# Turning five of seven FFT blocks by DMA instead of on TensorE, in the backward pass of a two-layer SSM and MLP kernel

## The chip, the cores and the metric

The kernel runs on one core of a Trainium2 chip. The core has a matrix engine (PE, with its weight loads shown as PEld), a vector engine (DVE), a scalar engine (ACT), a general engine (POOL) and a sequencer that only issues transfers (SP). SP, ACT and POOL each issue DMAs to a queue of their own; all queues share 16 DMA engines. The metric is the time of one execution on the device in microseconds (us); lower is better.

## The reference, cut to what matters

The reference is a two-layer network and the gradients of its eight inputs. Each layer is an SSM block (a short shift convolution, a product, a long convolution by FFT, a gate) and a SiLU MLP, both behind a layer norm and a residual. All arrays are bf16, with sequence length S = 2048, width D = 448 and hidden width F = 1792.

```python
def _A_ref(q, k, v, shift_k, ssm_k, ssm_D):
    ...
    kv = k_shift * v
    ...
    y_f = kv_f * kf_f[None, :, :, :]
    y = irfft2(y_f, s=(1, L))[:, 0, :S, :]
    y = y + kv * ssm_D[None, None, :]
    return q * y
...
x = x + _A_ref(_layernorm(x), A_k, A_v, A_shift_k, A_ssm_k, A_ssm_D)
x = x + _B_ref(_layernorm(x), B_w1, B_w2)
x = x + _A_ref(_layernorm(x), A_k, A_v, A_shift_k, A_ssm_k, A_ssm_D)
x = x + _B_ref(_layernorm(x), B_w1, B_w2)
...
_out, _vjp = jax.vjp(_f, A_q, A_k, A_v, A_shift_k, A_ssm_k, A_ssm_D, B_w1, B_w2)
```

The outputs are the forward result and the eight gradients. Both layers share their weights, so the gradient of `y`, the output of the long convolution, is summed over the layers and goes back through the FFT once, at the end.

## The kernel before, in words

The program has three parts. `_ssm_prefix` computes the forward long convolution. `Main.run` goes over four chunks of 512 positions and does the forward and backward of both layers; along the way it stores the operands of the weight gradients, turned, in DRAM (`OP_d`, keys a and g per layer), and the normalised inputs n1 and n3 (`N_d`). `_ssm_suffix` takes the gradient of `y` back through the FFT. The change lies in the suffix.

**Stages of the suffix.** Stage 1 of the FFT (`_fft_stage1`, L214) multiplies the 16 rows of the output gradient (`Ysb`) by a matrix and copies the results into the tile A1 (`A1g`); the last four rows run at L1165. Stage 2 needs each 128x128 block of A1 turned. The loop at L1185 does this for seven groups of sixteen blocks: `_turn64` (L222) issues 32 matmuls with the identity into a PSUM tile of the tag `mm`, and a copy (L1189) brings the result to `Z[g]`, a part of the tile `B1v`. DVE or ACT does the copy, by the balancer `_Bal.pick`, which keeps a running total of costs for each. Then `spectrum(cp)` (L1193) does stage 2 on `Z[cp]` at L236 and copies it back on ACT (L1199), and DVE makes a copy with halves swapped (L276). `inverse(cp, ...)` (L1204) forms products with the stored spectra on DVE (L1212, L1213) and runs the first inverse stage (L265), in two chunks per `cp`. Its results go to `B1k`, which is a view of A1's own memory with another layout, and to `B1v_`, each by a copy on ACT (L116). A chunk of `B1k` is a strided set of elements that runs through all of A1. `spec_load(cp)` (L1174) loads the stored spectra on POOL's queue; two buffers rotate for even `cp`, others serve odd `cp`.

**Jobs.** The weight gradients are computed by `Jobs`, a generator whose steps are four matmuls each (L1046). The suffix puts `jobs.run(n)` between its own stages, to keep PE busy. One job run takes a stationary operand `dstat` (512 KB) and does 16 matmuls, against `go` or `X` (L1046, operands a) or against n3 and n1 (operands g). `load` (L1027) issues the DMA for `dstat` from SP's queue at L1038; four buffers rotate. `load_n3` (L1104) loads n3 (1.8 MB) by SP at L1107; it is placed behind the last `dstat` load that the program has issued by then (`issue_after`). A finished weight block is copied by ACT (L1115) and stored by POOL (L1116).

**Order.** PE's order is the program's order, written by hand (`manual_schedule`). On the other engines and queues a planner sets the order, from its own estimate of when each instruction is ready; on the chip each of them then works strictly in that order. Waits are put in where tiles overlap.

Two other places of the kernel turn by DMA, both on SP's queue: L426 in the prefix (two groups of a like tile, SBUF to SBUF) and L595 in `Main.store`.

Of the kernel before, what the change touches and what calls it, by code (L numbers as in the profile page):

```python
# [11 lines left out]
BF16 = mybir.dt.bfloat16  # L12
# [5 lines left out]
P = 128  # L18
# [73 lines left out]
class _Bal:  # L92

    def __init__(self, nc):
        self.nc = nc
        self.load = {"act": 0.0, "dve": 0.0}
# [17 lines left out]
def _copy(nc, eng, out, in_):  # L114
    if eng is nc.scalar:
        return nc.scalar.copy(out, in_)  # L116
    return eng.tensor_copy(out, in_)  # L117
# [18 lines left out]
def kernel(  # L136
# [63 lines left out]
    with tc.manual_schedule(engines={nc.tensor.engine}):  # L200
        with ExitStack() as es:
            Main(k, es).run(ys)
        _ssm_suffix(k)


def _hd(k, shape, name):
    return k.hd.tile(shape, BF16, name=name, tag="hd", bufs=3)


def _load_minv(k, eng):  # L210
    eng.dma_start(out=k.Minvsb[:].rearrange("p n c k -> p (n c k)"), in_=k.minv_h.ap())
# [10 lines left out]
def _turn64(k, pt, i, src):  # L222
    for r in range(2):
        rs = slice(64 * r, 64 * r + 64)
        k.nc.tensor.transpose(pt[:, r, i, :], src[rs], k.ident[rs, rs])
# [776 lines left out]
class Jobs:  # L1002


    def __init__(self, k, main):
        self.k, self.nc, self.main = k, k.nc, main
        self.hd = False
        self.n_ld = self.n_bank = self.n_st = 0
        self.pend = None

    def gen(self):
# [15 lines left out]
    def load(self, key, ft, hd=False):  # L1027
        k, nc = self.k, self.nc
        i = self.n_ld
        self.n_ld += 1  # L1030
        if hd or (self.hd and i % 5 == 4):
            st = _hd(k, [P, NT, P], "dstat")[:]
        else:
            st = self.stat[:, self.n_st % 4]
            self.n_st += 1
        src = k.OP_d[key]
        if key in k.TURNED:
            self.last_ld = nc.sync.dma_start(out=st, in_=src[:, ft, :, :])  # L1038
        else:
            nc.sync.dma_start_transpose(out=st, in_=src[ft, :, :])  # L1040
        return st
# [104 lines left out]
def _ssm_suffix(k):  # L1146
    nc, tc, bal = k.nc, k.tc, k.bal
    jobs = k.jobs
    k_pm = _pm(k.A_k[0])
    v_pm = _pm(k.A_v[0])  # L1150
    psum = k.psum
    mm = dict(tag="mm", bufs=2)
    k.pt = dict(s1=mm, s2=mm, v=mm)
    A1 = k.A1g
    with ExitStack() as es:
# [12 lines left out]
        Z = [B1v_[:, 16 * g:16 * g + 16, :] for g in range(7)]  # L1168
# [3 lines left out]
        A1f = A1[:].rearrange("p a c n s -> p (a c n s)").rearrange("p (a b) -> p a b", b=P)  # L1172

        def spec_load(cp):  # L1174
            lo, hi = cp * 2048, (cp + 1) * 2048
            if cp % 2:
                kk = [kk1[:, i] for i in range(2)]
            else:
                kk = [sp.tile([P, 2048], BF16, name="kk_d", tag="gK", bufs=2)[:] for i in range(2)]
            nc.gpsimd.dma_start(out=kk[0], in_=k.SPEC_d["K"][:, lo:hi])  # L1180
            k.last_sp = nc.gpsimd.dma_start(out=kk[1], in_=k.SPEC_d["KV"][:, lo:hi])
            return kk

        kks = [spec_load(0)]
        for g in range(7):  # L1185
            pt = psum.tile([P, 2, 16, 64], BF16, name="ps_tr", **mm)
            for i in range(16):
                _turn64(k, pt, i, A1f[:, 16 * g + i, :])
            _copy(nc, bal.pick(2048, dve_ns=0.53), Z[g].rearrange("p i (r x) -> p r i x", r=2), pt[:])  # L1189
            jobs.run(1)  # L1190
        kks.append(spec_load(1))

        def spectrum(cp):  # L1193
            xsw = _hd(k, [P, 2048], "xsw_c")
            kk = kks[cp]
            zs = [Zf[cp][:, u * 1024:(u + 1) * 1024] for u in range(2)]
            jobs.run(2)
            for z, ps in zip(zs, _fft_stage2(k, zs, psum)):
                k.last_x = nc.scalar.copy(z, ps[:])  # L1199
            jobs.run(2)  # L1200
            _swap_halves(k, xsw, Zf[cp])
            return kk[0], kk[1], xsw

        def inverse(cp, t):  # L1204
            for u in range(2):
                ci = 2 * cp + u
                o = slice(u * 1024, (u + 1) * 1024)
                prods = []
                for spec_t in (t[1], t[0]):
                    pa, pb = pab[:, 0, n_p[0] % 3], pab[:, 1, n_p[0] % 3]  # L1210
                    n_p[0] += 1
                    nc.vector.tensor_tensor(out=pa, in0=Zf[cp][:, o], in1=spec_t[:, o], op=ALU.mult)  # L1212
                    nc.vector.tensor_tensor(out=pb, in0=t[2][:, o], in1=spec_t[:, o], op=ALU.mult)  # L1213
                    bal.add("dve", 1.9)
                    prods.append((pa, pb))
                jobs.run(6 - u)
                for (pa, pb), B1, cnd in zip(prods, (B1k, B1v_), (True, False)):
                    _fft_inv_stage2_half(k, pa, pb, B1, ci, psum, cnd)

        prev = spectrum(0)  # L1220
        for cp in range(NCI // 2):
            cur = spectrum(cp + 1) if cp + 1 < NCI // 2 else None
            inverse(cp, prev)
            if cp + 2 < NCI // 2:
                kks.append(spec_load(cp + 2))
            prev = cur
            if cp == 0:
                with tc.issue_after(jobs.last_ld.ins):
                    jobs.load_n3()
            if cp == 1:  # L1230
                with tc.issue_after(k.last_sp.ins):
                    nc.gpsimd.memset(gks[:, 16:19, :], 0.0)
                    _load_minv(k, nc.gpsimd)
            if cp == 4:
                with tc.issue_after(k.last_x.ins):
                    nc.scalar.dma_start(out=gks[:, 0:16, :], in_=v_pm)
            if cp == 5:
                ksf = sp.tile([P, 2, J, D // 2], BF16, name="ksf")
                with tc.issue_after(k.last_x.ins):
                    nc.scalar.dma_start(out=ksf[:], in_=k.KS_d[:].rearrange("h p j d -> p h j d"))  # L1240
                skx = ws[:, 0:8 * D].rearrange("p (a b) -> p a b", a=2)
                nc.scalar.dma_start(out=skx[:, 0, :], in_=k.A_shift_k.rearrange("d j -> (d j)").partition_broadcast(P))
                skb = skx[:, 1, :].rearrange("p (j d) -> p j d", j=4)
                nc.vector.tensor_copy(skb, skx[:, 0, :].rearrange("p (d j) -> p j d", j=4))
# [130 lines left out]
```

## Time and profile before

| what | value |
|---|---|
| median of 3 runs | 702.56 us (701.79 to 702.73) |
| profiled execution | 701.8 us |
| its span, first to last instruction | 700.0 us |
| PE busy | 666.0 us, 95% of the span |
| DVE, ACT, POOL busy | 484.1, 432.9, 101.3 us |
| granted TensorE clock | 0.998 |
| bytes by DMA, mean rate | 161.03 MB, 230 GB/s |
| turns in the suffix, L225 | 224 matmuls, 515.6 to 524.7 us |

The profile is of one execution. Its timelines give the start of an instruction in us from the span's start, its duration, and in brackets how long the engine had been idle and what ended that. A name such as `ps_tr<-ident,A1g` is output tile, then inputs. Matmuls are pipelined, so a line's duration reaches over the start of the next; the distance between starts is the time that a group takes. For a DMA the duration is that of issuing it, and its landing is given beside it.

### The profile page before, as it was taken

To read this page: it belongs to the slowest core of one execution; us is meant where nothing else is said; L and a number is where in the kernel's file an instruction comes from. 1 tells how busy PE (TensorE), PEld (TensorE's weight loads), DVE (VectorE), ACT (ScalarE), POOL (GpSimd) and SP (SyncE) were. 2 spreads that over 40 slices of the span, in tenths; PEclk is the share of its full clock that TensorE was granted. 3 is DMA by queue.
4 is the path that set the end of the run, shared out by engine and by line. 5 is a ranking of instruction groups with operands and counts; after the bars stand their busy time and mean duration, and the time that the engine had idled before them with its cause. 6 is when DMAs were issued, how large, how long until landed. Compare 5 with 4: busy or idle time off the path is not lost.

```text
span 700.0 us, 14553 instructions
## 1 busy us (share of the span) xinstructions
PE 666.0 (95%) x5897; PEld 358.8 (51%) x5933; DVE 484.1 (69%) x1131; ACT 432.9 (62%) x522; POOL 101.3 (14%) x173
## 2 busy tenths in 40 slices
PE   6898789999999999999999999999999999999996
PEld 5876545454444444434444444544554555555664
DVE  6688862676889948899578874853946545538991
ACT  5888766968856857769577585223554553554431
POOL 1057110110011100111000100010111211102311
PEclk9999999999999999999999999999999999999999
DMA  8999938459899976698677799959557888966981
GB/s 321 270 298 306 376 84 210 118 107 243 219 231 249 246 200 166 146 240 221 185 165 194 194 242 329 262 172 229 177 208 280 307 279 307 352 188 215 331 293 42
DMA packets 199798, 161.03 MB, mean 230 GB/s; under 512 B 147698, under 2 KB 180213, under 8 KB 198963
## 3 DMA queue, kind: packets, MB, share of 16 engines
q1 hardware_dynamic: 184550, 111.78, 58.8%
q0 software_dynamic: 10368, 36.29, 15.3%
q10 hardware_dynamic: 4812, 12.04, 5.0%
q8 instruction: 46, 0.75, 0.4%
q14 instruction: 22, 0.17, 0.1%
HBM read 66.05 MB, written 54.60 MB: 172 GB/s over the span
## 4 chain that ended last, share of the span: by engine, by line
PE 57%; DVE 22%; issue 10%; ACT 5%; POOL 3%; DMA 2%; POOLq 0%; DVEq 0%; ACTq 0%
PE ps_d L1046 19%; PE ps_n L836 8%; PE ps_h L638 6%; PE ps_g L638 6%; PE ps_o L798 5%; DVE ln_st L301 2%; DVE lb_v L994 2%; PE ps_v L265 2%; PE ps_cv L449 2%; POOL rstd L306 2%; DVE n L309 1%; DVE lb_v L997 1%; DVE lb_v L998 1%; DVE X L802 1%; PE ps_h L642 1%
## 5 line engine op out<-in xcount | busy, mean ns | idle before, releaser
L1046 PEld LDWEIGHTS <-dstat 128*128 128x128 bf16 x896 | 84.0, 98 | 77.8 <-issue 4.0
L836 PE MATMUL ps_n<-w1T,ghT 128*128 128x448 bf16 x448 | 96.6, 353 | 2.0 <-DVE ghT L821 1.7
L798 PE MATMUL ps_o<-w2sb,aT 128*128 128x448 bf16 x448 | 89.2, 353 | 0.7 <-DVE X L802 0.7
L638 PE MATMUL ps_h<-nT,w1sb 128*128 128x512 bf16 (+1 forms) x410 | 83.5, 336 | 2.2 <-ACT Dall L116 1.0
L116 ACT CAST ghT<-ps_g 128x1024 bf16<-128x1024 f32 (+1 forms) x54 | 48.4, 899 | 58.4 <-PE ps_g L642 47.7
L638 PE MATMUL ps_g<-nT,w2T 128*128 128x512 bf16 x317 | 77.9, 379 | 2.2 <-DVE Dall L117 0.5
L836 PEld LDWEIGHTS <-ghT 128*128 128x128 bf16 x448 | 41.4, 98 | 50.7 <-DVE ghT L821 6.7
L798 PEld LDWEIGHTS <-aT 128*128 128x128 bf16 x448 | 43.2, 98 | 41.1 <-issue 2.8
L638 PEld LDWEIGHTS <-w1sb 128*128 128x128 bf16 x420 | 39.2, 98 | 36.7 <-issue 7.2
L781 ACT ACTIVATE aT<-ps_h 128x1024 bf16<-128x1024 f32 (+1 forms) x48 | 44.2, 921 | 19.4 <-PE ps_h L638 10.5
L116 ACT CAST Dall<-ps_h 128x1024 bf16<-128x1024 f32 (+2 forms) x60 | 54.3, 904 | 0.0
L994 DVE SCALAR_TENSOR_TENSOR lb_v<-lb_u,n 128x448 bf16<-128x448 bf16 x60 | 37.2, 620 | 24.6 <-ACT lb_u L840 24.1
L791 ACT ACTIVATE Dall<-Dall 128x1024 bf16<-128x1024 bf16 (+1 forms) x48 | 53.2, 1186 | 0.1
L638 PEld LDWEIGHTS <-w2T 128*128 128x128 bf16 x336 | 31.3, 98 | 42.1 <-issue 7.2
L306 POOL TENSOR_TENSOR rstd<-ln_ve,mhalf 128x2 f32<-128x2 f32 (+1 forms) x24 | 19.9, 831 | 221.1 <-DVE ln_ve L305 221.1
L1046 PE MATMUL ps_d<-X,dstat 128*128 128x448 bf16 x224 | 47.9, 353 | 0.0
L1046 PE MATMUL ps_d<-go,dstat 128*128 128x448 bf16 x224 | 47.2, 353 | 0.0
L1046 PE MATMUL ps_d<-n3m,dstat 128*128 128x448 bf16 x224 | 46.4, 353 | 0.0
L1046 PE MATMUL ps_d<-n1m,dstat 128*128 128x448 bf16 x224 | 46.3, 353 | 0.0
L840 ACT ACTIVATE lb_u<-ps_n,rstd 128x448 bf16<-128x448 f32 x32 | 20.5, 640 | 28.7 <-PE ps_n L836 24.3
L116 ACT CAST A1g<-ps_v 128x1024 bf16<-128x1024 f32 x14 | 14.9, 1066 | 36.5 <-PE ps_v L265 36.5
L802 DVE TENSOR_TENSOR X<-X,ps_o 128x448 bf16<-128x448 bf16 x32 | 19.5, 610 | 21.3 <-PE ps_o L798 21.1
(206 smaller groups left out, 1111.6 us busy)
## 6 DMA issues: line engine op xcount, KB each, us to landing
dstat<-a_d SPq DMA_DIRECT2D x28, 512.0 KB, 5.0
dstat<-g_d SPq DMA_DIRECT2D x28, 512.0 KB, 5.2
a_d<-turned SPq DMA_DIRECT2D x16, 512.0 KB, 3.0
g_d<-turned SPq DMA_DIRECT2D x16, 512.0 KB, 3.2
a_d<-turned SPq DMA_DIRECT2D x16, 384.0 KB, 2.7
g_d<-turned SPq DMA_DIRECT2D x16, 384.0 KB, 3.0
spec_K<-KAB POOLq DMA_DIRECT2D x7, 512.0 KB, 5.4
KAB<-KAB POOLq DMA_DIRECT2D x28, 128.0 KB, 4.6
```

Source lines behind the costliest of these rows:

```text
L116: return nc.scalar.copy(out, in_)
L265: nc.tensor.matmul(pv[:, r ^ (ci & 1), i, :], lhsT=src[ri, i * P:(i + 1) * P], rhs=k.Gsb[ri, g, ri], start=first, stop=not first)
L306: nc.gpsimd.tensor_tensor(out=r[:, lo:hi], in0=ve[:, lo:hi], in1=k.mhalf[:, lo:hi], op=ALU.pow)
L638: self.nc.tensor.matmul(ps, lhsT=w[:, b, ft * P:(ft + 1) * P], rhs=x[:, b], start=(start and b == 0), stop=(stop and b == bs[2]))
L781: self.last_silu = nc.scalar.activation(aT[hh][:, o:o + hi - lo, :], ps(lo, hi), ACT.Silu)
L791: self.nc.scalar.activation(dT[hh][:, o:o + n, :], dT[hh][:, o:o + n, :], ACT.Derivative_silu)
L798: nc.tensor.matmul(po[:, :D], lhsT=aT[ft // 7][:, ft % 7, tl * P:(tl + 1) * P], rhs=self.w2sb[:, ft, :], start=(ft == 0), stop=(ft == NF - 1))
L802: self.last_o = nc.vector.tensor_tensor(out=X[:, t, :], in0=X[:, t, :], in1=po[:, :D], op=ALU.add)
L836: nc.tensor.matmul(pn[:, :D], lhsT=gh[ft // 7][:, ft % 7, tl * P:(tl + 1) * P], rhs=self.w1T[:, ft, :], start=(ft == 0), stop=(ft == NF - 1))
L840: nc.scalar.activation(u0[:], pn[:, :D], ACT.Identity, scale=k.rstd[2 * L + 1][:, t:t + 1], accum_out=cp[:, tl, 0:1])
L994: nc.vector.scalar_tensor_tensor(out=v[:], in0=u0, scalar=-1.0 / D, in1=n_t, op0=ALU.mult, op1=ALU.mult, accum_out=cp[:, 1:2])
L1046: self.nc.tensor.matmul(ps[:, :D], lhsT=st[:, t, :], rhs=mov[:, t, :], start=(first and t == 0), stop=(last and t == NT - 1))
```

## The change

The groups 2 to 6 of A1 are turned by five DMA transposes on SP's queue, issued ahead of the loop; the matmul turns and their PSUM copies stay for groups 0 and 1. The loop still runs seven job steps. From there until the end of the first pass of the inverse loop, `dstat` loads go to POOL's queue instead of SP's; after that pass they go to SP's again. The load of n3 is issued after the second pass instead of the first.

```diff
@@ class Jobs, __init__
         self.n_ld = self.n_bank = self.n_st = 0
+        self.queue = k.nc.sync
         self.pend = None
@@ Jobs.load
         if key in k.TURNED:
-            self.last_ld = nc.sync.dma_start(out=st, in_=src[:, ft, :, :])
+            self.last_ld = self.queue.dma_start(out=st, in_=src[:, ft, :, :])
@@ _ssm_suffix
         kks = [spec_load(0)]
+        jobs.queue = nc.gpsimd
+        for g in range(2, 7):
+            nc.sync.dma_start_transpose(out=Z[g], in_=A1f[:, 16 * g:16 * g + 16, :].rearrange("p a b -> p (a b)"))
         for g in range(7):
-            pt = psum.tile([P, 2, 16, 64], BF16, name="ps_tr", **mm)
-            for i in range(16):
-                _turn64(k, pt, i, A1f[:, 16 * g + i, :])
-            _copy(nc, bal.pick(2048, dve_ns=0.53), Z[g].rearrange("p i (r x) -> p r i x", r=2), pt[:])
+            if g < 2:
+                pt = psum.tile([P, 2, 16, 64], BF16, name="ps_tr", **mm)
+                for i in range(16):
+                    _turn64(k, pt, i, A1f[:, 16 * g + i, :])
+                _copy(nc, bal.pick(2048, dve_ns=0.53), Z[g].rearrange("p i (r x) -> p r i x", r=2), pt[:])
             jobs.run(1)
...
             if cp == 0:
+                jobs.queue = nc.sync
+            if cp == 1:
                 with tc.issue_after(jobs.last_ld.ins):
                     jobs.load_n3()
-            if cp == 1:
                 with tc.issue_after(k.last_sp.ins):
```

## The prediction

> **What bounds the kernel now.** I read the page's chain of waits first, then the PE timeline around the change, then the queues beside it. The chain:
>
> ```profile
> PE 57%; DVE 22%; issue 10%; ACT 5%; POOL 3%; DMA 2%; POOLq 0%; DVEq 0%; ACTq 0%
> ```
>
> It is an average over stages. What a change at L1185 to L1190 is worth is read in that stage, in PE's timeline (start, duration, what):
>
> ```profile
> 514.04 1.68 PE L1046 MATMUL ps_d<-go,dstat 128*128 128x448 bf16 x8
> 515.65 0.64 PE L225 MATMUL ps_tr<-ident,A1g 64*128 64x64 bf16 x32
> 516.23 0.93 PE L1046 MATMUL ps_d<-go,dstat 128*128 128x448 bf16 x4
> 517.09 0.64 PE L225 MATMUL ps_tr<-ident,A1g 64*128 64x64 bf16 x32
> ...
> 524.27 0.64 PE L225 MATMUL ps_tr<-ident,A1g 64*128 64x64 bf16 x32
> 524.85 2.44 PE L1046 MATMUL ps_d<-go,dstat 128*128 128x448 bf16 x12
> 527.22 0.63 PE L236 MATMUL ps_s<-B1v,Gsb 64*64 64x512 bf16 x8
> ```
>
> No idle time stands behind any line: the seven turns and the job matmuls between them follow one another. The table by stretches says the same of what follows (start:end, length, busy PE, PEld, DVE, ACT, POOL, clock, DMA share, GB/s):
>
> ```profile
> 515.20:523.00 7.80, 7.80 (x195) 4.41 (x195) 3.67 (x3) 2.81 (x3) 0.04 (x1) 1.00 0.61 220
> 523.00:531.00 8.00, 8.00 (x108) 4.00 (x105) 3.27 (x5) 5.27 (x5) 0.55 (x1) 1.00 0.42 116
> 531.00:537.00 6.00, 6.00 (x38) 2.94 (x39) 5.88 (x9) 2.36 (x3) 0.54 (x1) 1.00 0.99 404
> ```
>
> PE is full, at full clock, and stays so until 694.9. Its order is written by hand. So work taken out of PE here brings the end nearer by as much, as long as every operand still comes in time: PE, with nothing spare, is also where each late operand shows.
>
> **What goes.** From one turn to the next is 1.435 us (516.23, 517.66, 519.10 and so on for the job matmuls). Four job matmuls without a turn take 0.757 us (16 in 3.03 us, 532.23 to 535.26). So a turn and its two changes of shape cost 0.68 us, and five cost 3.4 us; by the turn's share of the chain alone (0.575 us) it is 2.9. I take 3.4. Five PSUM copies go as well, three on DVE of 1.22 us and two on ACT of 1.87 us. They end no wait of PE, so they are worth nothing; the balancer's totals stand 0.75 us apart before and 0.66 after, so later copies fall to the same engines.
>
> The second half of the kernel hangs on PE's progress: the DVE stretch from 630.6 to 682 begins at a matmul's result, and its loads and stores at PE and DVE events. All of it moves forward together. The tail from 694.9 is unchanged.
>
> **What comes: five transposes on SP.** Each turns 128x2048. Two lines issue that shape:
>
> ```profile
> L595 SPq DMA_TRANSPOSE turned<-aT x32: 1339/1624/3752, 113.7 to 417.4; - x32
> DMA to landing us min/median/max: 3.2/4.0/9.0
> ...
> L426 SPq DMA_TRANSPOSE KAB<-KAB x2: 3603/4920/6238, 20.2 to 26.5; - x2
> DMA to landing us min/median/max: 5.7/8.0/10.4
> ```
>
> (L595's figures mix in blocks of three quarters of the size.) They can start when the last stage-1 copy ends, at 515.2. From below: of two issued one behind the other (306.89 and 308.58) the second, of three quarters, landed 1.37 us after the first, so 1.83 us for a full one; five land by 515.6 + 3.7 + 4 x 1.83 = 526.7. From above: each waits for the one before, at the shorter of L426's two, 5.66 us: 515.6 + 28.3 = 543.9. (The 10.4 us of its first contains loads already queued on SP, the last landing at 26.56.) The five need some 9.2 us of all the DMA engines. Shares of 0.61 and 0.42 leave 7.7 us free by 531, and n3's load, which filled 531 to 537, is gone from there. Loads that now come 3.4 us earlier take some back. I take 531 to 533.
>
> Who needs them? Z[2] is read by PE at 545.28, now 541.9; Z[3] to Z[6] 14 us apart. Earlier is a need that the diff does not show: the first inverse writes A1, which all five transposes read, through B1k:
>
> ```profile
> 538.32 1.07 ACT L116 CAST A1g<-ps_v 128x1024 bf16<-128x1024 f32 x1 [4.33 <-PE ps_v L265]
> 539.28 1.02 ACT L116 CAST B1v<-ps_v 128x1024 bf16<-128x1024 f32 x1
> ...
> 543.25 1.07 ACT L116 CAST A1g<-ps_v 128x1024 bf16<-128x1024 f32 x1 [2.52 <-PE ps_v L265]
> ```
>
> That ACT copy now wants to start at 534.9 and must wait for all five. Behind it on ACT are the B1v copy, a dout copy and the next pair. PE meets the wait when it wants the two `mm` banks for the second inverse chunk, at 542.6 - 3.4 = 539.2; the two copies take 2.0 us, so a landing by 537.2 costs nothing and each us after it one us. I cost it at zero, hidden by 4 us of margin; without that cover it is up to 543.9 - 537.2 = 6.7 us.
>
> **What moves: six dstat loads to POOL.** By PE's runs of 16 they are those used from 519.10, 524.85, 528.54, 532.23, 535.26 and 539.43. Four buffers rotate, so each may be issued when the run four earlier ends: 505.9, 510.1, 513.9, 518.6 and, with the shift, 521.4 and 525.3. Used 3.4 us earlier (the first 0.7), they have 12.5, 11.3, 11.2, 10.2, 10.5 and 10.7 us. POOL's own loads of that size:
>
> ```profile
> kk_d<-spec_K POOLq DMA_DIRECT2D x4, 512.0 KB, 5.7
> kk_d<-spec_KV POOLq DMA_DIRECT2D x4, 512.0 KB, 6.7
> ```
>
> They cost 0.54 us of issue each, 3.2 us in all on an engine that is idle here, and land with 3 us or more to spare. From the other side: 11.82 us, the slowest of them (issued at 589.08), would make each up to 1.6 us late. I take zero. Queued on POOL beside them are dout stores, which wait for ACT for under a us once their run is done, and the second spectrum's load, which waits until 538.5 for DVE:
>
> ```profile
> 534.28 0.54 POOL L1116 DMA_DIRECT2D out_dram<-dout  x1 [8.53 <-ACT dout L1115]
> 538.77 0.54 POOL L1180 DMA_DIRECT2D kk_d<-spec_K  x1 [3.95 <-DVE pab L1213]
> ```
>
> All six can go out well ahead of that load, if the planner puts them there. The next dstat load, on SP from about 529, queues behind transposes instead of beside n3 and is used at 540.2: 11 us.
>
> **What moves: n3.** It goes to SP after the last load of the next pass, about 539.7 instead of 529.16. It landed in 9.2 us; its first use is 577.58, now 574.2. It cannot be late itself. But 1.8 MB, some 4 us of DMA time, enter a stretch with shares of 0.81 to 1.0 (539 to 561). Loads behind it there had 3 to 4 us of spare (issued 550.57, landed 558.84, used 562.5). It is spread over four loads: zero, at worst some 2 us.
>
> **The sum.** Profiled execution: 701.8 us, of which 700.0 is its span. 701.8 - 3.4 = 698.4. The median of three, 702.56, lies 0.76 above it, so 702.56 - 3.4 = **699.2 us** for the median.
>
> **Rivals.**
>
> *A. The overwrite of A1 waits* (slower). If the transposes land one after another, at 543.9, PE stands 6.7 us at the second inverse chunk: 699.2 + 6.7 = 705.9. It turns the gain into a loss from a landing at 540.6 on, that is at over 5.0 us per transpose. For it: L426's issues took 3.6 and 6.2 us, and dstat loads share the DMA engines. Against it: the pairs of L595 overlap. Chance 0.12.
>
> Here a rule of the Trainium skill speaks against the change: the page "VectorE: DVE Perf Modes", section "The three transpose paths", gives a DMA transpose of 128x128 bf16 1309 ns and TensorE 390 ns. As an estimate from that page, a block of sixteen would take 20.9 us and five would land at 620, some 83 us too late. The trace does not agree: sixteen in one DMA land in about 4 us. So that form of A gets 0.01 of its 0.12.
>
> *B. POOL's order* (slower). If the planner puts the last job load behind the second spectrum's, it is issued at 535.9 at the earliest and lands 5.7 us later, at 541.6; PE wants it at 536.0. That is 5.6 us: 704.8. Nothing in the profile shows the new order; for it only that POOL works strictly in order, against it that the load is free ten us earlier. Chance 0.07.
>
> *C. Crowded DMA* (gain partly lost). POOL loads at 11.8 us, transposes landing at 538 to 540, or n3 among the loads around 550 take 1 to 3 us: 700.2 to 702.2. Chance 0.14.
>
> That the change does nothing can be left out: the diff takes matmul turns and copies out under one condition.
>
> **How the numbers follow.** Forecast 0.67 (698.4 to 700.0), C 0.14, A 0.12, B 0.07. Forecast and C hold 0.81, so the range is 698.4 to 702.2; A and B lie beyond it. About 0.2%, 1.4 us, is what a measurement of this kernel can tell from no change. Faster than 701.15: the forecast and nearly half of C, 0.73. Within: the rest of C, 0.08. Slower than 703.97: 0.19.
>
> **What would show it.** Right: two turns at L225 instead of seven, `spectrum`'s first L236 at about 523.8, no idle PE time up to 560, the first A1g copy after it on ACT still released by PE, last transpose landed by 537. Wrong: that copy released by a DMA of B1v and PE idle before the second L265 (A); PE idle at L1046 with POOL waiting at L1180 (B); PE idle at L1046 with dstat landings over 9 us (C).

## The result, and the profile after

The changed kernel takes 709.5 us (median of 6 runs, 705.9 to 717.7); the kernel before took 702.7 us (701.8 to 703.2) in the same rounds. The ratio is 1.0081, 95% interval [1.0056, 1.0106]: slower, where 699.2 us had been forecast. Ratios leave out executions more than 1.5% above the fastest of the same kernel (here one of six, at 717.7 us); medians and ranges take in all. The profiled execution of the changed kernel took 709.26 us, 707.3 of it the span. Its lines lie one or two below those of before: L1047 for the job matmuls, L1188 for the transposes, L1039 for `dstat` loads.

The chain of waits has a new member, SP's queue at 3%, and a larger share of DMA:

```profile
PE 51%; DVE 21%; issue 10%; ACT 6%; DMA 4%; POOL 3%; SPq 3%; ACTq 0%; POOLq 0%; DVEq 0%
```

PE's timeline in the changed stage (start, duration, what, and in brackets the idle time before and what ended it) shows both the gain and the loss:

```profile
516.81 0.64 PE L225 MATMUL ps_tr<-ident,A1g 64*128 64x64 bf16 x32
517.38 0.93 PE L1047 MATMUL ps_d<-go,dstat 128*128 128x448 bf16 x4
518.25 0.64 PE L225 MATMUL ps_tr<-ident,A1g 64*128 64x64 bf16 x32
518.82 0.93 PE L1047 MATMUL ps_d<-go,dstat 128*128 128x448 bf16 x4
...
524.98 0.63 PE L236 MATMUL ps_s<-B1v,Gsb 64*64 64x512 bf16 x8
...
537.19 3.19 PE L1047 MATMUL ps_d<-go,dstat 128*128 128x448 bf16 x16
546.93 1.95 PE L265 MATMUL ps_v<-Gsb,pab 64*128 64x64 bf16 x64 [6.55 <-ACT A1g L116]
548.82 3.17 PE L1047 MATMUL ps_d<-X,dstat 128*128 128x448 bf16 x8
551.91 1.02 PE L236 MATMUL ps_s<-B1v,Gsb 64*64 64x512 bf16 x8
```

Two turns are left of seven, and `spectrum` starts at 524.98 instead of 527.22. Then PE stands for 6.55 us ahead of the second L265, and what follows is slow: eight job matmuls take 3.17 us (548.82) where before eight took 1.69. ACT's timeline names the cause:

```profile
531.19 0.55 ACT L1116 CAST dout<-ps_d 128x448 bf16<-128x448 f32 x1
545.87 1.02 ACT L116 CAST A1g<-ps_v 128x1024 bf16<-128x1024 f32 x1 [14.12 <-DMA B1v<-A1g]
546.78 1.02 ACT L116 CAST B1v<-ps_v 128x1024 bf16<-128x1024 f32 x1
```

The first copy into A1's memory, released by a PE matmul before, is now released by a DMA of B1v that reads A1: the last transpose, landed at 545.69. On SP's queue (start, time of issuing) the five transposes hold everything behind them:

```profile
516.45 27.14 SPq L1188 DMA_TRANSPOSE B1v<-A1g  x5
543.71 1.93 SPq L1039 DMA_DIRECT2D dstat<-a_d  x4
545.69 0.54 SPq L1108 DMA_DIRECT2D n3m<-N_d  x1
```

The table by stretches (start:end, length, busy PE, PEld, DVE, ACT, POOL, granted clock, DMA share, GB/s) gives the stall and what comes behind it. The DMA share adds up the times of packets, which overlap, so it can pass 1. The last stretches:

```profile
531.00:537.00 6.00, 6.00 (x91) 3.39 (x90) 5.89 (x10) 0.75 (x2) 1.02 (x2) 1.00 1.50 226
537.00:540.30 3.30, 3.30 (x18) 1.57 (x16) 1.64 (x3) 0.00 (x0) 0.58 (x2) 1.00 0.82 181
540.30:546.90 6.60, 0.08 (x1) 0.09 (x1) 0.00 (x0) 1.03 (x2) 0.00 (x0) 0.67 1.06 282
546.90:552.80 5.90, 5.87 (x80) 2.99 (x79) 2.50 (x4) 3.20 (x4) 2.60 (x4) 0.50 1.05 431
```

In 540.3 to 546.9 ACT's copies at the end are nearly all the work that is done; in 546.9 to 552.8 PE is busy throughout, at half the clock. The granted clock is half from 542.5 to 552.8, 10.24 us.

**Where the time went.** Equal instructions set against the profile of before are 1.16 us late ahead of the changed stage (this arises in the first 90 us, in code that is the same), 2.24 us early after the turns, 4.38 us late at the second inverse chunk, and 7.04 us late from 552 on. So the sum is 701.8 + 1.16 (the start) - 3.40 (the turns) + 6.62 (the stall) + 2.66 (half clock) = 708.84; 0.42 of the 709.26 is spread over the rest and the time around the span.

### The profile page after: what moved, and what is told of

It reads as the page before. It is cut to its first block, busy times and chain, and to the rows that moved or that the text cites. A ratio compares the mean times of both kernels' runs of the same rounds, so it can differ in the third digit from the quotient of the medians.

```text
span 707.3 us, 14249 instructions
## 1 busy us (share of the span) xinstructions
PE 668.8 (95%) x5737; PEld 360.4 (51%) x5773; DVE 480.7 (68%) x1128; ACT 429.0 (61%) x520; POOL 104.2 (15%) x179
## 4 chain that ended last, share of the span: by engine, by line
PE 51%; DVE 21%; issue 10%; ACT 6%; DMA 4%; POOL 3%; SPq 3%; ACTq 0%; POOLq 0%; DVEq 0%
PE ps_d L1047 15%; PE ps_n L836 8%; PE ps_h L638 6%; PE ps_g L638 6%; PE ps_o L798 5%; SPq L1188 3%; DVE ln_st L301 2%; DVE lb_v L994 2%; PE ps_v L265 2%; POOL rstd L306 2%; PE ps_cv L449 2%; ACT KAB L116 1%; DVE n L309 1%; DVE lb_v L997 1%; DVE lb_v L998 1%
## 5 line engine op out<-in xcount | busy, mean ns | idle before, releaser
L1047 PEld LDWEIGHTS <-dstat 128*128 128x128 bf16 x896 | 84.7, 98 | 79.6 <-issue 5.6
L1047 PE MATMUL ps_d<-X,dstat 128*128 128x448 bf16 x224 | 48.9, 361 | 0.0
L1047 PE MATMUL ps_d<-go,dstat 128*128 128x448 bf16 x224 | 47.2, 353 | 0.0
L1047 PE MATMUL ps_d<-n3m,dstat 128*128 128x448 bf16 x224 | 46.4, 353 | 0.0
L1047 PE MATMUL ps_d<-n1m,dstat 128*128 128x448 bf16 x224 | 46.3, 353 | 0.0
```

The lines of the kernel that those rows point to most:

```text
L1047: self.nc.tensor.matmul(ps[:, :D], lhsT=st[:, t, :], rhs=mov[:, t, :], start=(first and t == 0), stop=(last and t == NT - 1))
```

## The experiments

The theory after this result: the transposes are slow because POOL's `dstat` loads run beside them; they then stop PE in two ways, by the overwrite of A1 and by the loads that stand behind them on SP. The rivals: transposes of this kind are slow by themselves; or the moved loads, or n3, cost something of their own.

**1. The moves without the transposes.** Loads on POOL and the later n3 as in the change, all seven turns on PE.

```diff
-        for g in range(2, 7):
-            nc.sync.dma_start_transpose(out=Z[g], in_=A1f[...])
...
-            if g < 2:
```

> The kernel before, with only the queue and n3 parts of the change: six job loads on POOL, n3 one pass later, all seven blocks turned on PE. Theory (contention between transposes and POOL's loads): without transposes there is nothing to starve, the loads land in 5 to 8 us with ten to spend: no difference, 702 to 703.5. Rival (the queue move or the later n3 costs time by itself): slower by 1 us or more, with PE idle at a job matmul.

703.2 us (10 runs, 702.6 to 704.2), ratio 0.9997 [0.9986, 1.0008]. No idle time of PE in the stage; the trace is 1.32 us late from the start and stays so to the end. Without the transposes, the moved loads and n3 cost nothing.

**2. The transposes without loads beside them.** The six POOL loads are left out, so PE multiplies what its buffers happen to hold and the weight gradients are not computed from the right operands; PE's work is the same.

```diff
-            self.last_ld = self.queue.dma_start(out=st, in_=src[:, ft, :, :])
+            if self.queue is nc.sync:
+                self.last_ld = nc.sync.dma_start(out=st, in_=src[:, ft, :, :])
```

> The changed kernel without the six job loads that it issues on POOL (PE works on what the buffers still hold, so the weight gradients of these runs are not the reference's); everything else is unchanged. Theory (contention): the five transposes have the DMA engines to themselves but for the two spectrum loads until 521 and a few stores; the last lands by about 530, no wait of ACT on a DMA, PE has no idle time, and the full 3.4 us are gained: 698.7 to 700.3. Rival (slow by themselves): the last transpose lands at 540 or later, PE idles at the second inverse chunk, 704 to 709.

699.4 us (699.3 to 701.2), ratio 0.994 [0.992, 0.996]: faster. Against the profile of before the trace goes from 2.58 us late to 0.81 early over the turns, 3.40 us, and keeps it; PE has no idle time. The transposes' issues (min/median/max ns) and landings here, and then in the changed kernel:

```profile
L1189 SPq DMA_TRANSPOSE B1v<-A1g x5: 1427/1937/4530, 517.9 to 529.5; - x5
...
DMA to landing us min/median/max: 4.4/5.5/6.0
```

```profile
L1188 SPq DMA_TRANSPOSE B1v<-A1g x5: 3327/5438/7560, 516.5 to 538.2; - x5
...
DMA to landing us min/median/max: 7.5/10.2/12.9
```

Issued over 11.6 us instead of 21.7, the last landing at 533.9 instead of 545.7. "Slow by themselves" falls: from the first issue to the last landing the five take 16.0 us here, 29.2 in the changed kernel.

**3. All loads on SP.** The transposes alone on the queue, no second one beside them but POOL's spectrum loads and stores.

```diff
-        jobs.queue = nc.gpsimd
```

> The changed kernel with one part undone: all job loads stay on SP's queue (the five transposes and the later n3 stay). Theory (contention): the transposes are slow because POOL's loads run beside them in another queue; without these they land by about 531, the first copy into A1 is released by PE and not by a DMA. But two or three job loads now stand behind the transposes on SP, are issued near 528 instead of 520 and land near 533, where PE wants the first at 530: PE idles 3 to 4 us at a job matmul instead of 6.6 us at the inverse. Time 702.5 to 705.5. Rival (the transposes are slow by themselves, 5 to 6 us each in turn): they land near 545 as before, the loads behind them near 550, PE idles some 20 us; time over 718.

708.8 us (707.5 to 709.0), ratio 1.0069 [1.0045, 1.0093]. The transposes are fast, 2.5 us apart, the last landed at 534.06, and there is no wait at L265. But the stall is there, at another place. SP's queue, then PE:

```profile
507.52 8.26 SPq L1039 DMA_DIRECT2D dstat<-a_d  x3
516.91 14.87 SPq L1187 DMA_TRANSPOSE B1v<-A1g  x5
531.89 10.89 SPq L1039 DMA_DIRECT2D dstat<-a_d  x5
```

```profile
536.27 6.16 PE L1047 MATMUL ps_d<-go,dstat 128*128 128x448 bf16 x16 [5.67 <-DMA dstat<-a_d]
```

The loads that PE needs next stand behind five transposes. The idle time of 5.67 us was expected at 3 to 4, and the half clock behind it (from 535.5 on, 6.83 us) was not expected at all, nor a time over 705.5: kind right, size missed. So the move of the loads to POOL had a reason, and it is that move which slows the transposes.

**4. The overwrite taken away.** The first two chunks of `B1k` go to an idle part of another tile; DVE copies them to A1 after the second pass.

```diff
+        side = ws[:, 4096:6144].rearrange("p (q d) -> p q d", d=64)
...
-                    _fft_inv_stage2_half(k, pa, pb, B1, ci, psum, cnd)
+                    _fft_inv_stage2_half(k, pa, pb, side if cnd and ci < 2 else B1, ci, psum, cnd)
...
+                nc.vector.tensor_copy(B1k[:, :, 0:64], side)
```

> The changed kernel with the overwrite taken away: the first two inverse chunks of the one half are put in 4 KB per partition that lie idle then, and copied into A1 by one DVE copy in the second pass, so the first copy on ACT needs no transpose to be done. All five transposes and the POOL loads stay as they are. Theory (the overwrite of A1 is what makes PE wait): the transposes land as late as before (529 to 546) but nobody waits, since Z[2] is wanted at 543 and the others later; PE has no idle time, its clock stays full: 698.8 to 700.5. Rival (late job loads, or the clock alone): PE still idles, 704 or more. If only the second need is late, Z[2] to Z[6] being behind, PE idles at the third stage-2 group.

709.0 us (701.8 to 714.4), ratio 1.0068 [1.0038, 1.0098]: no better. The wait at L265 is gone, and the next one stands behind it, 9 us on:

```profile
541.76 1.11 PE L265 MATMUL ps_v<-Gsb,pab 64*128 64x64 bf16 x64
...
550.88 3.17 PE L1047 MATMUL ps_d<-X,dstat 128*128 128x448 bf16 x8 [8.01 <-DMA dstat<-a_d]
```

```profile
517.50 28.00 SPq L1189 DMA_TRANSPOSE B1v<-A1g  x5
545.62 1.93 SPq L1039 DMA_DIRECT2D dstat<-a_d  x4
```

The four loads behind the transposes go out at 545.6 although their buffers come free from about 531.5 on (three groups, below, issue the first of them at 531.54). In the changed kernel this second wait is hidden in the first: both end when SP is done. The expectation had overlooked it.

**5. Is it POOL's queue?** The six loads on ACT's queue.

```diff
-        jobs.queue = nc.gpsimd
+        jobs.queue = nc.scalar
```

> The change with the six dstat loads issued from ACT's queue instead of POOL's, at the places that the planner gives them among ACT's copies. Theory (any second queue with 4 KB packets holds up the 256-byte packets of the transposes): landings stay 5 to 6.5 us apart, PE stalls 4 to 7 us at the second inverse chunk, 706 to 711 us. Rival (it is POOL's queue, whose transfers the trace lists as software ones, that starves a hardware queue; two hardware queues share well): landings 2.5 to 4 us apart, the last by 537, no stall there, 699.5 to 703 us, with up to 1 us of ACT waiting for buffers in either case.

708.4 us (four runs, 704.5 to 713.3), ratio 1.0106 [1.0069, 1.0144]. In the profiled run, the fastest of the four, the transposes land at 525.26, 530.15, 535.13, 538.75 and, by ACT's release, 542.3: 4.9 us apart while loads are about, 3.6 at the end. PE stands before L265:

```profile
543.42 0.64 PE L265 MATMUL ps_v<-Gsb,pab 64*128 64x64 bf16 x32 [2.99 <-ACT A1g L116]
544.33 0.64 PE L265 MATMUL ps_v<-Gsb,pab 64*128 64x64 bf16 x32 [0.27 <-ACT B1v L116]
```

From the first landing to the last that is 4.3 us each, as beside POOL's loads (4.2; 528.87 to 545.69) and far from the 2.5 of experiment 3: a second queue of either kind does it. From the first issue to the last landing the five take 25.8 us here and 29.2 beside POOL's loads, and the stall, 3.26 us, is below the 4 to 7 expected; but the other three runs took 708 to 713 us, so it is not shown that ACT's queue is the milder one. The granted clock was half behind this stall too, for 3.41 us.

**6. The loads in smaller pieces.** Each POOL load as two DMAs of interleaved pieces of 1 KB.

```diff
-            self.last_ld = self.queue.dma_start(out=st, in_=src[:, ft, :, :])
+            if self.queue is nc.gpsimd:
+                src = src[:, ft, :, :]
+                for y in range(2):
+                    cut = lambda t: t.rearrange("p (x y b) f -> p x y (b f)", x=2, y=2)[:, :, y, :]
+                    self.last_ld = nc.gpsimd.dma_start(out=cut(st), in_=cut(src))
...
```

> The change, with each of POOL's six dstat loads split into two DMAs whose rows are cut into pieces of 1 KB instead of 4 KB (12 DMAs in all, the same bytes). Theory (the queues take turns packet by packet on each DMA engine, so a 256-byte packet of a transpose waits for one packet of POOL's queue each time): the packets of the loads become shorter, the transposes get more turns in the same time, land 3 to 5 us apart instead of 5.9, and PE's stall at the second inverse chunk shrinks from 6.6 us to 0 to 4: 704 to 708 us where the changed kernel takes 709.5. Rival (the DMA engines share by bytes, or the transposes are held up by something that has nothing to do with the loads' packets): landings stay 5.5 to 6.5 us apart and the time at 708.5 to 711.

715.9 us (714.3 to 722.2), ratio 1.0187 [1.0136, 1.0238]. The trial did not do what it was meant to: POOL's packets still have 4,096 bytes in the trace, so it says nothing on the length of a turn. There are twice the DMAs; the six of them that are issued from 519.0 on land in 11 to 15 us, where the loads beside transposes took 7 to 9. PE waits for them twice, 2.17 and 0.80 us, and the transposes are held up more than ever (landings 535.9 to 558.4):

```profile
559.63 1.95 PE L265 MATMUL ps_v<-Gsb,pab 64*128 64x64 bf16 x64 [15.25 <-ACT A1g L116]
```

**7. The number of groups.** Four, three and two groups by DMA, loads on POOL as in the change; and three with all loads on SP. The edit for three, against the changed kernel:

```diff
-        for g in range(2, 7):
+        for g in range(4, 7):
...
-            if g < 2:
+            if g < 4:
```

> The change for four groups (3 to 6) by DMA, loads on POOL: the point between three groups, which gain, and five, which lose. Theory (transposes land 5 to 6 us apart beside POOL's loads, and each us that the last lands after about 539 is a us of PE at the second inverse chunk): the first three as in the three-group run, to 536 or so, the fourth at 541 to 543, PE idle 2 to 4 us before the second L265, released by ACT's A1g copy; four turns of 0.68 us are 2.7 us off and 2 to 4 back, 702 to 705 us against 703 to 703.9 before, plus up to 2.7 if the idle time is long enough for half clock. Rival (the loss comes at once with the fifth, from something not proportional): no idle time there, 700.3 to 701.

> The change for three groups (4 to 6) by DMA instead of five, loads on POOL as in the change. Three turns of 0.68 us go: 2.0 us. Theory (each transpose beside POOL's loads takes 5.9 us, and the second inverse chunk waits for the last): the third lands at about 540, 0 to 2 us after the A1g copy wants to start, with PE idle 0 to 2 us and no slower clock, and the next dstat loads get out by 538: 701 to 703.5 us against 703 before. If the stall of the changed kernel came from something other than the number of transposes, idle time of 4 us or more stays and the time is 706 to 708.

> The change for two groups (5 and 6) by DMA, loads on POOL. Two turns of 0.68 us go, 1.36 us, and by the three-group run nothing comes back: 701 to 702.5 us against 703 to 703.9 before, 0.4 to 0.8 us more than three groups; the transposes land by 534 and the A1g copy is released by PE. If three groups were already held back by something that two are not, two would be as fast or faster.

> Three groups (4 to 6) by DMA, and all dstat loads on SP as before the change. Theory (transposes alone land 2.5 us apart; what stops PE with five of them on SP is that the next dstat loads stand behind them, issued from 531.9 on): the transposes land by 530, the loads behind them are issued from about 527 on, 5 us earlier than with five, PE's idle time at L1047 falls from 5.67 us to 0 to 1, and the time is 701 to 702.5 us against 703 before (2.0 us less, and up to 0.7 back). Rival (a dstat load behind any transpose on SP is late): idle 3 us or more, 704 to 707.

| by DMA | loads on | median us (range) | ratio to before | last landing | PE idle |
|---|---|---|---|---|---|
| 5 (the change) | POOL | 709.5 (705.9 to 717.7) | 1.0081 [1.0056, 1.0106] | 545.7 | 6.55 |
| 4 | POOL | 703.3 (699.6 to 716.0) | 0.9991 [0.9962, 1.002] | 540.9 | 1.15 at L265, 0.85 at L1047 |
| 3 | POOL | 701.9 (701.2 to 702.6) | 0.997 [0.9958, 0.9981] | 536.0 | none |
| 2 | POOL | 701.7 (700.7 to 702.8) | 0.9983 [0.9968, 0.9997] | 527.7 | none |
| 3 | SP | 702.0 (700.4 to 705.0) | 0.9978 [0.9964, 0.9992] | 532.2 | 0.77 |

Landings and idle times are those of the profiled run. In it the turns give 2.72 us for four groups, 2.03 for three and 1.36 for two (2.04 for three on SP): 0.68 each every time. With three, ACT's copy is released by PE again, 1.4 us after the last landing; with four, by the DMA, at 541.06. ACT of three, then of four:

```profile
537.44 1.07 ACT L116 CAST A1g<-ps_v 128x1024 bf16<-128x1024 f32 x1 [4.33 <-PE ps_v L265]
```

```profile
541.06 1.02 ACT L116 CAST A1g<-ps_v 128x1024 bf16<-128x1024 f32 x1 [8.44 <-DMA B1v<-A1g]
```

Three groups on SP have the other wait, at its edge:

```profile
533.52 3.20 PE L1047 MATMUL ps_d<-go,dstat 128*128 128x448 bf16 x16 [0.77 <-DMA dstat<-a_d]
```

The stall with four came out smaller than expected (1.15 us, not 2 to 4). In the profiled runs the gain goes by the number of groups, and the loss sets in with the landing, as the theory has it. The times show less: the intervals of the three kernels with two or three groups overlap, and four can't be told from no change, with runs from 699.6 to 716.0 us.

**8. Transposes spread between the loads on SP.** Two ahead of the loop, one after the load that follows it, two after the load in the first inverse chunk; no loads on POOL.

```diff
-        jobs.queue = nc.gpsimd
-        for g in range(2, 7):
...
+        turn((2, 3))
...
+                if (cp, u) == (0, 0):
+                    with tc.issue_after(jobs.last_ld.ins):
+                        turn((5, 6))
...
+            if cp == 0:
+                with tc.issue_after(jobs.last_ld.ins):
+                    turn((4,))
```

> All five groups by DMA and all dstat loads on SP, but the transposes are spread: two ahead of the loop, one after the load that follows the loop, two after the load issued in the first inverse chunk. Theory (no loads beside the transposes, and no load behind more than two of them): transposes 2.5 to 3 us each; the last lands at 537 to 540, so the second inverse chunk waits 0 to 3 us; no idle time over 2 us for a dstat load; 699.6 to 703 us against 703 before. Rival (the transposes and loads can't share the stretch in any order, 9 us of transposes and the loads being more than it holds): idle time of 4 us or more in one place, a slower clock behind it, 705 to 709.

707.7 us (702.2 to 709.2), ratio 1.0037 [1.0013, 1.0062]: the rival's outcome. The last transpose landed at 539.35, before PE met it; but four loads went out together behind it from 536.3 on, beside two spectrum loads of POOL, and the first took 8.27 us:

```profile
544.64 5.59 PE L1047 MATMUL ps_d<-go,dstat 128*128 128x448 bf16 x16 [6.80 <-DMA dstat<-a_d]
```

**9. Both waits taken away.** The idle tile of experiment 4, and the four loads that stood behind the transposes issued from ACT's queue, n3 a pass later.

```diff
             if cp == 0:
-                jobs.queue = nc.sync
+                jobs.queue = nc.scalar
...
+            if cp == 1:
+                jobs.queue = nc.sync
+                nc.vector.tensor_copy(B1k[:, :, 0:64], side)
```

> The change with both waits of PE taken away: the first two chunks of B1k go to an idle part of another tile (copied to A1 by DVE after the second pass), and the four dstat loads that stood behind the transposes on SP are issued from ACT's queue at about 532 to 542, so that SP holds the transposes alone; n3 follows a pass later. Theory (the overwrite of A1 and the loads queued behind the transposes are the only two waits, and the half clock follows from them): no idle time of PE over 1.5 us, full clock, 699 to 702 us, although the transposes land late (by 550). Rival (the DMA engines can't hold transposes and loads in that stretch whatever the queue): the four loads land 9 us or more after their issue, PE idle 3 us or more at L1047 or a transpose later than 555 stops the second pass, 704 to 709.

Four runs, at 701.3, 722.9, 725.6 and 734.3 us: too far apart for a ratio. The profile is of the one at 722.9. In it the loads on ACT's queue land 9.9, 15.0 and 22.0 us after their issue (the fourth's landing isn't in the trace), the last transpose at 571.9, and PE stands in several places:

```profile
560.32 3.17 PE L1047 MATMUL ps_d<-X,dstat 128*128 128x448 bf16 x8 [3.95 <-DMA dstat<-a_d]
573.06 1.04 PE L265 MATMUL ps_v<-Gsb,pab 64*128 64x64 bf16 x32 [3.41 <-ACT A1g L116]
```

With three queues at work loads and transposes got slower still: in the profiled run that is the rival's mechanism. The other three runs have no profile here, neither the two at 725.6 and 734.3 nor the one at 701.3, which is in the range of the theory. What decides between the two outcomes stays open, and so does whether the two waits were the only ones.

## Why the prediction was wrong

**The step that failed** is the transposes' landing: "I take 531 to 533." It came from 9.2 us of DMA time set against 7.7 us of free share by 531. They landed at 545.69, beyond even the upper bound of 543.9. The last one landed 29.2 us after the first issue, where 531 to 533 allowed 15.4 to 17.4. That much five transposes took without those loads (16.0 us in experiment 2) or with them on their own queue (17.2 in experiment 3): in effect the forecast left the loads beside them no time.

The trace's DMA packets show what the sum lacked. In these 29.2 us the packets of other transfers took 14.7 us of each DMA engine. Five transposes at their quickest pace would take 9.2 (5 x 1.83), and those of their packets that took over 0.2 us, 119 in number, took 6.6 more: 30.5 in all, some of it overlapping, so hardly any time of the engines was left unused. The 6.6 us stood at nothing in the sum (they are 1.7 us in experiment 2, without the loads). And the other transfers took 10.4 us from 516.4 to 532.2, where the profile of before has 8.0 from 515.2 to 531.0.

How the queues share shows in the packets by queue (packets, MB, share of 16 engines by packets that start there; q0 is POOL's, q1 SP's). From 528 to 529, then from 531 to 532, both have packets under way:

```profile
q0 software_dynamic: 79, 0.31, 90.2%
q1 hardware_dynamic: 29, 0.01, 8.0%
```

```profile
q0 software_dynamic: 75, 0.27, 66.5%
q1 hardware_dynamic: 105, 0.03, 21.7%
```

From 540 to 542, beside the second spectrum's load:

```profile
q0 software_dynamic: 163, 0.60, 98.6%
q1 hardware_dynamic: 21, 0.00, 0.6%
```

Here q1's 21 packets have 4 bytes each: no transpose moves data, and the fifth, issued at 538.15, sends its first packet at 542.52. A transpose of 512 KB is 2,048 packets of 256 bytes, 18 ns each in the median; a load's packets have 4,096 bytes and take 159 ns. Nearly alone, the transposes moved 1,247 packets in 2 us (532 to 534). The Trainium skill, page "DMA: Bandwidth & Descriptors", section "Queues, rings and completion order", says that each DMA engine takes turns between queues, a packet at a time. As an estimate from that rule and the two durations, with each record of the trace taken for such a packet, a transpose would get 18 of every 177 ns, a tenth. The trace agrees roughly where both have packets under way, 8.0% and 21.7%, but the rule does not account for the wait up to 542.52. Experiments 2, 3 and 5 show the contention itself; that the length of a packet is its cause is argued from these rows, and experiment 6, meant to show it, did not.

**The steps that hang on it.** "I cost it at zero, hidden by 4 us of margin": the cover was gone. What the wait then costs was put at up to 6.7 us; it was 6.6. The kind of wait was right; that the number fits is partly luck, as two misses cancel. Without the late start of 1.16 us the landing, 544.53, is 0.6 us past the bound, and PE went on after the first of ACT's two copies, 1.0 us, not after 2.0. Rival A is thus what happened, with this price but without the clock (below); its threshold, over 5.0 us per transpose, was passed with 5.9 (516.45 to 545.69 for five). It had a chance of 0.12, mainly because the pairs at L595 overlap. Those pairs had no large loads beside them on a second queue. In experiment 2, without the loads, the first two landed 1.83 us apart, the figure taken from L595, but the other three took 2.9 us each on average: the reading was right for a pair, and did not carry to five in a row, still less to a place with other traffic.

**"The next dstat load, on SP ... 11 us"** failed too. It went out at 543.71, not at about 529 as supposed, because SP issues in order and each transpose's issue lasted 3.3 to 7.6 us. In the changed kernel that costs nothing visible, as PE already waits; experiments 3 and 4 show it as a wait of 5.67 and 8.01 us. Taking away the overwrite alone gave nothing back (experiment 4).

**Not in the sum at all: the clock.** After PE had stood from 540.4, the granted clock went to half at 542.5 for 10.24 us, and 2.66 us more were lost. The same followed 5.67 us of idle time in experiment 3 and, for 3.41 us, 3.26 us in experiment 5; after the 1.15 us with four groups the clock stayed full. The Trainium skill, page "TensorE: Matmul & The Clock Gate", Part 1 on the clock gate, describes a monitor that looks at PE's activity in windows of about 3.4 us and grants half the pulses after an idle one. The trace agrees on the length: 10.24 us is three times 3.41, and experiment 3's 6.83 us twice. It does not agree that PE must be idle for a whole window: the clock went to half 2.1 us after PE stopped (540.4), and in experiment 5 after less than 3.4 us of idle time. A stall of 6.6 us was thus a loss of 9.3.

**What was right.** PE bounds the stage, and five turns are worth 3.40 us: measured 3.40, and 0.68 per turn in every variant. The six loads on POOL went out in good time (507.6 to 526.8) and landed in 4.0 to 8.6 us, some slower than the 5.7 and 6.7 read before but never late for PE; rival B's order did not come about. n3 and the moved loads cost nothing without the transposes (experiment 1). Rival C, crowded DMA, named the cause, and late transposes among what it would bring; but it had them land at 538 to 540, for 1 to 3 us, and they landed at 545.7.

**The base.** The profiled execution of before was among the fastest; the later profiles start 0.06 to 2.58 us behind it in unchanged code, which moves a sum by up to 0.4% before the change begins.

## What to carry to other kernels

A transfer that is short by itself can take nearly twice as long beside another queue's loads (here 29.2 us for five transposes against 16.0): read its duration from a place with the same traffic, and multiply it by the number of transfers that one wait collects. When work goes from a full engine to a queue, list everything behind it on that queue and everything that overwrites its source, and move only as much as lands before the first of these; here three groups of five, 701.9 us against 703.9 in the same rounds, ratio 0.997 [0.9958, 0.9981]. A wait removed can have a second one right behind it, ended by the same event.

## What the runs showed of the hardware that was not expected

- Where a queue with 256-byte packets and one with 4,096-byte packets (18 ns and 159 ns per packet in the median) both had packets under way, the first got 8 and 22% of the DMA engines, the second 90 and 67% (changed kernel, 528 to 529 and 531 to 532). From first issue to last landing five transposes took 29.2 us beside loads on POOL's queue, 25.8 beside loads on ACT's in its fastest run, and 16.0 without.
- In the same stretches some of the 256-byte packets take far longer than 18 ns: 119 over 0.2 us in the changed kernel, up to 1.9 us, together 6.6 us of each engine; 22 such packets and 1.7 us without the loads. What holds them is open.
- With several queues at work executions of one program scatter: three groups stay within 1.4 us, four spread from 699.6 to 716.0, experiment 4 from 701.8 to 714.4, experiment 9 from 701.3 to 734.3. What makes them scatter is open.
- Splitting a load into two strided DMAs of 1-KB pieces left its packets at 4,096 bytes and slowed both queues.
- Half clock came 2.1 us after PE stopped in the changed kernel and lasted 10.24 us; in experiment 3 it came 4.9 us after and lasted 6.83 us; in experiment 5, where PE stood for less than 3.4 us, it came 1.8 us after PE's work had resumed and lasted 3.41 us.
